# One-bank PSUM memories, ScalarE copies and an earlier search in a fused convolution and expert kernel

## The chip, the cores and the metric

The kernel runs as one launch on one core of a Trainium2 chip. The metric is the device time of an execution in microseconds (us). Five engines have an instruction queue of their own, each in order: TensorE (PE in the profile, its weight loads PEld), VectorE (DVE), ScalarE (ACT), GpSimd (POOL) and SyncE (SP), which issues nearly all transfers. Matrix products land in PSUM, which has eight banks of 512 fp32 numbers per partition; all other data lie in SBUF.

## The reference: a long convolution, then an expert for 128 rows

```python
Xf = np.fft.rfft(x, n=L, axis=1)            # x: 8 x 6336 x 128, L = 2 * 6336
y = np.fft.irfft(Xf * np.fft.rfft(h, n=L, axis=0)[None], n=L, axis=1)[:, :S, :]
...
scores = np.einsum('bsd,d->bs', y, w_gate)
top_idx = np.argpartition(-scores[b], 128)[:128]          # per batch b
ye = np.maximum(y[b, top_idx] @ w1, 0.0) @ w2             # 128 -> 1024 -> 128
out[b, top_idx] = y[b, top_idx] + sigmoid(scores)[:, None] * ye
```

Each of 128 channels is convolved with its own filter along 6336 positions. In each of the 8 batches the 128 positions of highest score then get a gated two-layer network added.

## The kernel before

6336 is 99 x 64, and the transforms are matrix products over the two factors. The work is cut into 8 **units** (`NU`): unit i holds two batches (pair i // 2) and half of the channels (i % 2). So an even unit and the odd one after it finish one pair. Each unit passes four stages, all in fp32:

- **A** (`stage_a`, L146): the n1 products, 8 groups, each two quarters q. A quarter is 16 matmuls into a PSUM tile `pb`, which two copies (L153 on ScalarE or L155 on VectorE, by a list of four flags) carry into the memory `ys`. Before it GpSimd folds the input (L133, L134, two operations a group).
- **B** (`stage_b`, L180, L189, L200): the n2 products, 13 chunks (12 of 8 columns, one of 3). A chunk is matmuls into `pb`, four VectorE multiplications with the filter's spectrum (L189) back into `ys` and a helper `tx`, and two GpSimd additions (L200). It needs a table chunk `wb` and a filter chunk `hd`, loaded three chunks ahead.
- **C** (`stage_c`, L262, L268): 66 steps s of up to four matmuls into `pa`, which ScalarE copies into `zs`. `zs` lies over the same memory as the unit's own `ys`.
- **D** (`stage_d`, L290, L295): 16 items of matmuls into `pa`, a ScalarE copy to `yt` and a store to the output.

Beside them runs the routing of each pair. `weigh` (L241) sums the 64 columns of a unit's `ys` with the gate's weights into `acc`, 64 VectorE operations. They are recorded inside stage C, up to five columns ahead of the step, and a copy into `zs` must wait for those whose columns it overwrites. When both units of a pair are summed, `scores` (L310) turns `acc` into scores; `pick` finds the 128th highest in 16 rounds, each a few VectorE operations (L356, L360, L363, L373) and one small matmul that sums counts over partitions (L368); then row numbers are made. When the pair's output is stored, `gather` (L458) fetches the rows by indirect transfers of GpSimd, and `feed` runs the network for the two batches (L469 to L497) and scatters the rows back.

**What sets the order.** The kernel is recorded under `manual_schedule`: each engine runs its instructions in the order in which the Python code makes them. The main loop over i takes 33 items: 17 from C (four steps each) and 16 from D. A table `plan` puts next unit's A ahead of items 1, 3, 5 and 7 (two groups each) and next unit's B ahead of items 10, 14, 18, 22, 26 and 30 (two chunks each, the last three). After each item `aside()` may advance the routing by one piece, if a modelled clock `t["pe"]` has passed the piece's due time (`after_dve`, `after_act`). The routing of a pair may start when the odd unit's C is over (`phase[1]`, item 17), and gather when the next unit begins. After unit 7 what is left of the routing runs alone.

PSUM is full: three one-bank `pa` buffers, two two-bank `pb` buffers and one bank `m` for the routing.

Of the kernel before, what the change touches and what calls it, by code (L numbers as in the profile page):

```python
# [32 lines left out]
def conv_moe(ctx, tc, x, h, wg_d, w1, w2, fa_d, wb_d, wc_d, at_d, wgl_d, tri_d, cst_d, tw_d, fb_d, out):  # L33
# [26 lines left out]
        return pa_.tile([128, 512], F32, tag="a", name="pa")  # L60

    def psb():
        return pb_.tile([128, 2, 512], F32, tag="b", name="pb")

    def psm():
        return pm_.tile([128, 512], F32, tag="m", name="m")
# [69 lines left out]
    def stage_a(g, r, engines):  # L136

        a, o = raw.pop(g), odd.pop(g)
        n = g % 8
        for q in range(2):  # L140
            pt = psb()
            for d in range(4):
                for b, c in ((0, 0), (1, 1), (0, 1), (1, 0)):
                    rows = slice(b * 64, b * 64 + NE)
                    src = (o if c else a[:, 0])[rows, q * 4 + d]
                    pe.matmul(pt[c * 64:c * 64 + 64, b, d * N1:(d + 1) * N1], src, fa[rows, c], start=True, stop=True)  # L146
            j = n * 4 + q * 2
            dst = ys[r].rearrange("p (b j) k t -> p b j t k", b=2)
            src = pt[:, :, 0:4 * N1].rearrange("p b (j t k) -> p b j t k", j=2, t=2)
            on_pe(0.7)  # L150
            for b in range(2):
                if engines[q * 2 + b]:
                    act.copy(out=dst[:, b, j:j + 2], in_=src[:, b])  # L153
                else:
                    v.tensor_copy(out=dst[:, b, j:j + 2], in_=src[:, b])  # L155
                    on_dve(0.5)

    kchunks = [(k, min(KC, N1 - k)) for k in range(0, N1, KC)]
# [44 lines left out]
    def stage_b(i, ci):  # L203
        r, u = i % 2, i % 2
        k0, kn = kchunks[ci]
        pt = psb()
        banks = [pt[:, 0], pt[:, 1]]
        over_k(r, wts.pop((r, ci)), ci, banks)
        ht = hts.pop((u, ci))
        times(r, ci, banks, [ht[:, 0, 0:kn], ht[:, 1, 0:kn]])  # L210
        load_w(r, ci + RW)
        load_h(u, ci + RH)

    def stage_b_first(ci):
# [7 lines left out]
        pt = psb()  # L222
        banks = [pt[:, 0], pt[:, 1]]
        over_k(0, wt, ci, banks)
        times(0, ci, banks, [hs[:, 0, 0, 0:kn], hs[:, 1, 0, 0:kn]])
        for u in range(2):
            sp.dma_start(out=hd[u, :, :, k0:k0 + kn], in_=hs[:, :, u, 0:kn])
        load_w(0, ci + RW)
# [11 lines left out]
        else:  # L240
            v.scalar_tensor_tensor(out=dst, in0=col, scalar=w, in1=dst, op0=ALU.mult, op1=ALU.add)  # L241

    def stage_c(i):
        r = i % 2
        y = ys[r].rearrange("p (j c) k t -> p j c k t", c=2)
        z = zs[r].rearrange("p (n g j) m t -> p n g j m t", g=2, j=2)
        banks = [None, None]
        weighed = 0
        for s in range(66):
            while weighed < min(64, s + 5):  # L250
                weigh(i, weighed)
                weighed += 1
            cols = [s, s - 2]
            for g in range(2):
                if 0 <= cols[g] < 64 and cols[g] % 4 == 0:
                    banks[g] = psa()
            for ri in range(2):
                for g in range(2):
                    c = cols[g]
                    if 0 <= c < 64:  # L260
                        rows = slice(g * 64, g * 64 + 64)
                        pe.matmul(banks[g][0:N1, c % 4 * 128:c % 4 * 128 + 128], y[rows, c // 2, ri, :, c % 2],  # L262
                                  wc[rows, ri], start=(ri == 0), stop=(ri == 1))
            on_pe(0.44)
            for g in range(2):
                c = cols[g]
                if 0 <= c < 64 and c % 4 == 3:
                    act.copy(out=z[:, c // 4, g].rearrange("p j m t -> p j t m"),  # L268
                             in_=banks[g][0:N1].rearrange("p (j t m) -> p j t m", j=2, t=2))
            if s % 4 == 3 or s == 65:  # L270
                yield

# [2 lines left out]
    def load_at(n):  # L275
        if n < 17:
            k = min(2, NT - 2 * n)
            ats[n] = tp.tile([N1, 2, 2, N1], F32, tag="at", name="at", bufs=RA)
            sp.dma_start(out=ats[n][:, 0:k], in_=at_d[:, 2 * n:2 * n + k])

    def stage_d(i):
        r, p, u = i % 2, i // 2, i % 2
        z = zs[r].rearrange("p j (c m) t -> p c m j t", c=2)
        for n in range(16):
            pt = psa()
            todo = [(0, 0, 1), (1, 1, 1), (2, 2, 2)] if n == 0 else [(2 * n + 1, 4 * n, 2), (2 * n + 2, 4 * n + 2, 2)]
            for tau, q, w in todo:
                o = q % 4 * 128
                for c in range(2):
                    pe.matmul(pt[0:N1, o:o + w * 128], ats[tau // 2][:, tau % 2, c], z[:, c, q:q + w],  # L290
                              start=(c == 0), stop=(c == 1))
                if tau % 2:
                    load_at(tau // 2 + RA)
            yt = tp.tile([N1, 2, 4, 64], F32, tag="y", name="yt", bufs=3)
            act.copy(out=yt.rearrange("p b q d -> p q b d"),  # L295
                     in_=pt[0:N1].rearrange("p (q b d) -> p q b d", q=4, b=2))
            on_pe(1.78)
            sp.dma_start(out=out[2 * p:2 * p + 2, u, :, 4 * n:4 * n + 4].rearrange("b a q d -> a b q d"), in_=yt)
            yield

# [163 lines left out]
    def feed(b0, got):  # L464
        ov = out[0:b0 + 2].rearrange("b u a q d -> (b u a q) d")
        for iu, xt in got:
# [11 lines left out]
            v.reciprocal(out=gg, in_=gg)  # L478
            hm = []
            for f0 in range(0, NF, 4):  # L480
                yield after_act(3.0)
                ph = psm().rearrange("p (f t) -> p f t", f=4)
                for f in range(4):
                    pe.matmul(ph[:, f], w1s[:, (f0 + f) * 128:(f0 + f + 1) * 128], xet, start=True, stop=True)  # L484
# [5 lines left out]
            yield after_act(3.0)  # L490
# [5 lines left out]
            for u in range(2):  # L496
                pool.indirect_dma_start(  # L497
                    out=ov, out_offset=bass.IndirectOffsetOnAxis(ap=iu[:, u:u + 1], axis=0),
                    in_=xt[:, u], in_offset=None)
            yield after_act(3.0)  # L500

    phase = [0, False]

    def route(p):
        b0 = 2 * p
        while phase[0] < 2 * p + 1 or not phase[1]:
            yield
        ss = yield from scores()
        picked = []
        yield from pick(b0, 2, ss, picked)  # L510
        while phase[0] < 2 * p + 2:
            yield
        got = gather(b0, picked)
        for n in range(4):
            yield
        yield from feed(b0, got)

    def all_routes():
# [10 lines left out]
    with tc.manual_schedule():  # L529
# [29 lines left out]
        fold(17, pool)  # L559

        for i in range(NU):
            phase[0], phase[1] = i, False
            if i < NU - 1:
                for ci in range(RW):
                    load_w((i + 1) % 2, ci)
            cs, ds = stage_c(i), stage_d(i)
            g0 = 16 + 8 * i
            plan = {}
            if i < NU - 1:
                for n in range(4):  # L570
                    plan.setdefault(1 + 2 * n, []).append(("a", 2 * n))
                for n in range(6):
                    plan.setdefault(10 + 4 * n, []).append(("b", 2 * n))
            for item in range(33):
                strand = cs if item < 17 else ds
                for kind, n in plan.get(item, []):
                    if kind == "a":
                        for g in (g0 + n, g0 + n + 1):
                            if g % 8 < 6:
                                fold(g + 2, pool)  # L580
                            elif g % 8 == 7:
                                fold(g + 1, pool)
                            stage_a(g, (i + 1) % 2, (1, 1, 0, 0))
                            load_x(g + RX)
                            if g % 8 == 7:
                                fold(g + 2, pool)
                    else:
                        for ci in (n, n + 1) if n < 10 else (10, 11, 12):
                            stage_b(i + 1, ci)
# [146 lines left out]
```

## Time and profile before

| what | value |
|---|---|
| three timed runs | 1099.97, 1106.51, 1111.1 us (median 1106.51) |
| the profiled execution | 1099.84 us; its span 1098.1 us, so 1.74 us lie around it |
| mean granted TensorE clock | 0.92 of full speed |
| start of unit 0's stage C | 116.3 us |
| end of unit 7's stage D | 1033.0 us |
| instructions | 39650 |
| moved by DMA | 170.81 MB, mean 156 GB/s |

The profile gives, for each engine, busy time and, for each idle stretch, the event that ended it. A group row reads: line, engine, operation, output<-inputs, shapes, count | busy us, mean ns of one | idle us before, and what ended it. A timeline row is start, duration, engine, line, operation, names, and in brackets the idle time just before. A fp32 matmul of the code is two MATMUL records in the profile (4096 of L262 for 2048 in the code); the instruction order counts it once.

### The profile page before, as it was taken

To read this page: it belongs to the slowest core of one execution; us is meant where nothing else is said; L and a number is where in the kernel's file an instruction comes from. 1 tells how busy PE (TensorE), PEld (TensorE's weight loads), DVE (VectorE), ACT (ScalarE), POOL (GpSimd) and SP (SyncE) were. 2 spreads that over 40 slices of the span, in tenths; PEclk is the share of its full clock that TensorE was granted. 3 is DMA by queue.
4 is the path that set the end of the run, shared out by engine and by line. 5 is a ranking of instruction groups with operands and counts; after the bars stand their busy time and mean duration, and the time that the engine had idled before them with its cause. 6 is when DMAs were issued, how large, how long until landed. Compare 5 with 4: busy or idle time off the path is not lost.

```text
span 1098.1 us, 39650 instructions
## 1 busy us (share of the span) xinstructions
PE 933.6 (85%) x17368; PEld 819.3 (75%) x17368; DVE 779.4 (71%) x1910; ACT 340.0 (31%) x619; POOL 481.6 (44%) x372
## 2 busy tenths in 40 slices
PE   5787799989998889988998789969998798999614
PEld 5687698879877787777877787769877697788514
DVE  5354777487778896787588796776768896791681
ACT  3522253235212431243223431234312441254101
POOL 7154754365335533654445443563436234420002
PEclk8899799999999999989999899989999898999856
DMA  6388545764466436563476346463465235513200
GB/s 254 118 269 281 190 136 159 250 221 136 132 210 196 135 117 221 153 206 100 125 229 200 114 124 202 149 207 109 134 196 166 93 89 183 173 51 98 87 0 10
DMA packets 102344, 170.81 MB, mean 156 GB/s; under 512 B 10814, under 2 KB 80028, under 8 KB 102172
## 3 DMA queue, kind: packets, MB, share of 16 engines
q1 hardware_dynamic: 101148, 167.24, 47.8%
q8 instruction: 136, 2.23, 0.8%
q0 software_dynamic: 1024, 1.05, 0.4%
q14 instruction: 36, 0.29, 0.1%
HBM read 135.29 MB, written 32.96 MB: 153 GB/s over the span
## 4 chain that ended last, share of the span: by engine, by line
PE 53%; DVE 36%; issue 5%; DMA 2%; ACT 2%; POOL 1%; POOLq 0%; ACTq 0%; SPq 0%; DVEq 0%
PE pa L290 14%; PE pa L262 13%; PE pb L180 12%; DVE acc L241 11%; PE pb L146 8%; DVE tx L189 6%; DVE slots L189 5%; DVE cmp L356 4%; DVE slots L155 2%; PE pa L180 2%; DVE num L360 2%; PE m L484 2%; PE m L493 2%; DVE r L363 1%; DMA out<-yt 1%
## 5 line engine op out<-in xcount | busy, mean ns | idle before, releaser
L200 POOL TENSOR_TENSOR slots<-slots,tx 128x512 f32<-128x512 f32 (+1 forms) x208 | 266.9, 1315 | 340.3 <-DVE tx L189 339.1
L262 PE MATMUL pa<-wc,slots 64*99 64x128 f32 x4096 | 276.5, 287 | 11.4 <-ACT slots L268 5.2
L262 PEld LDWEIGHTS pa<-wc,slots 64*99 64x99 f32 x4096 | 254.7, 177 | 24.8 <-issue 7.2
L290 PE MATMUL pa<-slots,at 99*99 99x256 f32 (+1 forms) x1056 | 244.3, 383 | 18.2 <-ACT slots L268 18.2
L241 DVE SCALAR_TENSOR_TENSOR acc<-slots,wgl,acc 128x198 f32<-128x198 f32 x496 | 241.4, 554 | 2.0 <-POOL slots L200 2.0
L268 ACT COPY slots<-pa 99x512 f32<-99x512 f32 x256 | 162.1, 634 | 244.9 <-PE pa L262 217.9
L180 PEld LDWEIGHTS pb<-slots 128*64 128x64 f32 x6336 | 198.7, 139 | 28.3 <-issue 18.4
L180 PE MATMUL pb<-slots 128*64 128x64 f32 x6336 | 207.4, 225 | 14.3 <-issue 9.0
L290 PEld LDWEIGHTS pa<-slots,at 99*99 99x99 f32 x1056 | 166.6, 167 | 68.8 <-ACT slots L268 19.9
L189 DVE TENSOR_TENSOR slots<-pb,ht 128x512 f32<-128x512 f32 (+1 forms) x182 | 119.4, 656 | 102.7 <-PE pb L180 95.7
L295 ACT COPY yt<-pa 99x512 f32<-99x512 f32 x128 | 75.0, 586 | 324.0 <-PE pa L290 191.3
L146 PE MATMUL pb<-fa,xr 50*64 50x99 f32 x2048 | 118.0, 263 | 55.1 <-DVE slots L155 43.5
L146 PEld LDWEIGHTS pb<-fa,xr 50*64 50x64 f32 x2048 | 100.9, 143 | 69.1 <-issue 46.7
L189 DVE TENSOR_TENSOR tx<-pb,ht 128x512 f32<-128x512 f32 (+1 forms) x182 | 118.8, 653 | 0.0
L155 DVE COPY slots<-pb 128x396 f32<-128x396 f32 x128 | 67.5, 564 | 66.7 <-PE pb L146 49.8
L153 ACT COPY slots<-pb 128x396 f32<-128x396 f32 x160 | 75.4, 524 | 68.3 <-PE pb L146 67.5
L133 POOL TENSOR_TENSOR two<-xr 128x512 f32<-128x512 f32 x42 | 55.4, 1319 | 62.8 <-PE pb L146 62.8
L134 POOL TENSOR_TENSOR xr<-xr 128x512 f32<-128x512 f32 x56 | 73.5, 1312 | 4.4
L146 PE MATMUL pb<-fa,two 50*64 50x99 f32 x1344 | 75.0, 258 | 0.0
L356 DVE SCALAR_TENSOR_TENSOR cmp<-r,q,quarters 99x192 bf16<-99x192 f32 x128 | 73.4, 614 | 0.3
L146 PE MATMUL pb<-fa,slots 50*64 50x99 f32 x1216 | 61.1, 293 | 11.9 <-DVE slots L134 8.3
L146 PEld LDWEIGHTS pb<-fa,slots 50*64 50x64 f32 x1216 | 53.1, 165 | 13.7 <-DVE slots L134 8.3
(100 smaller groups left out, 599.7 us busy)
## 6 DMA issues: line engine op xcount, KB each, us to landing
slots<-tab_wb SPq DMA_DIRECT2D x96, 512.0 KB
xr<-in_x SPq DMA_DIRECT2D x64, 512.0 KB
out<-yt SPq DMA_DIRECT2D x128, 198.0 KB
ht<-hd SPq DMA_DIRECT2D x84, 256.0 KB
at<-tab_at SPq DMA_DIRECT2D x128, 153.1 KB
hd<-slots SPq DMA_DIRECT2D x24, 256.0 KB
slots<-in_h SPq DMA_DIRECT2D x8, 512.0 KB
slots<-tab_wb SPq DMA_DIRECT2D x8, 192.0 KB
```

The source lines that it names most:

```text
L146: pe.matmul(pt[c * 64:c * 64 + 64, b, d * N1:(d + 1) * N1], src, fa[rows, c], start=True, stop=True)
L153: act.copy(out=dst[:, b, j:j + 2], in_=src[:, b])
L155: v.tensor_copy(out=dst[:, b, j:j + 2], in_=src[:, b])
L180: pe.matmul(banks[c][g * 64:g * 64 + 64, j * 64:j * 64 + 64], wt[:, j, c * 64:c * 64 + 64], y[:, :, g, :, k0 + j], start=True, stop=True)
L189: v.tensor_tensor(out=dst, in0=banks[c][:, 0:kn * 64].rearrange("p (k b j t) -> p k b j t", k=kn, b=2, t=2), in1=ht[t].rearrange("p k (j t ...
L200: pool.tensor_tensor(out=d3, in0=d3, in1=tx.rearrange("p k (j t) -> p k j t", t=2), op=ALU.add if c else ALU.subtract)
L241: v.scalar_tensor_tensor(out=dst, in0=col, scalar=w, in1=dst, op0=ALU.mult, op1=ALU.add)
L262: pe.matmul(banks[g][0:N1, c % 4 * 128:c % 4 * 128 + 128], y[rows, c // 2, ri, :, c % 2], wc[rows, ri], start=(ri == 0), stop=(ri == 1))
L268: act.copy(out=z[:, c // 4, g].rearrange("p j m t -> p j t m"), in_=banks[g][0:N1].rearrange("p (j t m) -> p j t m", j=2, t=2))
L290: pe.matmul(pt[0:N1, o:o + w * 128], ats[tau // 2][:, tau % 2, c], z[:, c, q:q + w], start=(c == 0), stop=(c == 1))
L295: act.copy(out=yt.rearrange("p b q d -> p q b d"), in_=pt[0:N1].rearrange("p (q b d) -> p q b d", q=4, b=2))
L356: v.scalar_tensor_tensor(out=cmp[:, j], in0=r[:, j].unsqueeze(1).broadcast_to([N1, 3, N2]), scalar=q[:, j:j + 1], in1=quarters[0:N1], op0= ...
```

## The change

1. `psb` gives two tiles of one bank each, with a name of its own per bank, in place of one tile of two banks. A, B and the prologue's B use them; the number of banks stays four.
2. In the main loop all four copies of an A group are on ScalarE (flags 1, 1, 1, 1); they were two on ScalarE and two on VectorE. The prologue's groups keep 1, 1, 1, 0.
3. The weighted sums of an odd unit leave its own stage C. They are recorded in the even unit before it, five after each item from 20 on, when that unit's items have already made all of the odd unit's B.
4. The routing of a pair may start at the beginning of the odd unit, no longer at its item 17.
5. B moves: in even units ahead of items 8, 10, 12, 14, 16, 17 (two chunks each) and 19 (one); in odd units ahead of 9, 13, 17, 20, 23, 26 (two each) and 29 (one).
6. `aside()` is called after every second step of C and inside every D item but the first, and no longer once per item. The due times of `feed` fall from 3.0 to 1.7 modelled us, a modelled 6.0 us stands between gather and feed in place of four items, and D's modelled cost is booked within the item.

```diff
     def psb():
-        return pb_.tile([128, 2, 512], F32, tag="b", name="pb")
+        return [pb_.tile([128, 512], F32, tag="b" + str(c), name="pb") for c in range(2)]
...
-                    pe.matmul(pt[c * 64:c * 64 + 64, b, d * N1:(d + 1) * N1], src, fa[rows, c], start=True, stop=True)
+                    pe.matmul(pt[b][c * 64:c * 64 + 64, d * N1:(d + 1) * N1], src, fa[rows, c], start=True, stop=True)
...
-        pt = psb()
-        banks = [pt[:, 0], pt[:, 1]]
+        banks = psb()
...
-    def stage_c(i):
+    def stage_c(i, weighing=True):
...
-            while weighed < min(64, s + 5):
+            while weighing and weighed < min(64, s + 5):
                 weigh(i, weighed)
...
+            if s % 2:
+                aside()
             if s % 4 == 3 or s == 65:
                 yield
...
+                on_pe(0.89)
+                if w == 2 and tau != 2:
+                    aside()
...
-            on_pe(1.78)
...
-                yield after_act(3.0)
+                yield after_act(1.7)
...
-        while phase[0] < 2 * p + 1 or not phase[1]:
+        while phase[0] < 2 * p + 1:
             yield
...
-        for n in range(4):
-            yield
+        yield after_act(6.0)
...
-            cs, ds = stage_c(i), stage_d(i)
+            cs, ds = stage_c(i, i % 2 == 0), stage_d(i)
...
-                for n in range(6):
-                    plan.setdefault(10 + 4 * n, []).append(("b", 2 * n))
+                for n, at_item in enumerate((8, 10, 12, 14, 16, 17, 19) if i % 2 == 0 else (9, 13, 17, 20, 23, 26, 29)):
+                    plan[at_item] = ("b", 2 * n, 2 if n < 6 else 1)
+            early = 0
...
-                            stage_a(g, (i + 1) % 2, (1, 1, 0, 0))
+                            stage_a(g, (i + 1) % 2, (1, 1, 1, 1))
...
-                if item == 17:
-                    phase[1] = True
+                if i % 2 == 0 and item > 19:
+                    for _ in range(5):
+                        if early < 64:
+                            weigh(i + 1, early)
+                            early += 1
                 next(strand, None)
-                aside()
```

Three places of the instruction order show it. Line numbers of the changed kernel are shifted a little: its L260, L239, L370, L397, L409, L417, L436 and L471 are L262, L241, L368, L395, L407, L415, L434 and L469 of the kernel before.

TensorE at the end of unit 7, before: the last D products (`pa<-slots,at`), then only the search's count sums.

```order
L368 LDWEIGHTS ones_87
L368 MATMUL m<-num,ones_87 99x6
L290 MATMUL pa<-slots,at 99x256 x4
L368 LDWEIGHTS ones_87
L368 MATMUL m<-num,ones_87 99x6
```

Fourteen further such pairs follow, and then the making of the row numbers. In the changed kernel the same place reads, with `cmp` and `lane` those of the row numbers and L471 the first instruction of `feed`:

```order
L290 MATMUL pa<-slots,at 99x256 x6
L436 LDWEIGHTS cmp
L436 MATMUL m<-lane_89,cmp 128x1
...
L290 MATMUL pa<-slots,at 99x256 x4
L436 LDWEIGHTS cmp
L436 MATMUL m<-lane_89,cmp 128x1
...
L438 MATMUL m<-hf,cmp 128x64
L471 MATMUL m<-tri,xe 128x128
L486 MATMUL m<-xet,w1s 128x128 x8
```

All 16 rounds of the last search now stand between earlier products of unit 7, and behind the last D product stand four small products for the second batch's row numbers.

VectorE in unit 0's stage C, where unit 1's A runs, before (`slots<-pb` are A's copies, `acc` the weighted sums):

```order
L239 TENSOR_SCALAR acc<-slots,wgl 128x198 x2
L241 SCALAR_TENSOR_TENSOR acc<-slots,wgl,acc 128x198 x6
L155 COPY slots<-pb 128x2x2x99 x4
L241 SCALAR_TENSOR_TENSOR acc<-slots,wgl,acc 128x198 x8
L155 COPY slots<-pb 128x2x2x99 x4
```

and now, through the first of five B pieces in the same stage:

```order
L237 TENSOR_SCALAR acc<-slots,wgl 128x198 x2
L239 SCALAR_TENSOR_TENSOR acc<-slots,wgl,acc 128x198 x30
L237 TENSOR_SCALAR acc<-slots,wgl 128x198 x2
L239 SCALAR_TENSOR_TENSOR acc<-slots,wgl,acc 128x198 x2
L189 TENSOR_TENSOR slots<-pb,ht 128x8x32x2
L189 TENSOR_TENSOR tx<-pb,ht 128x512
```

The copies are gone from this queue. Eight multiplications then alternate with eight sums three times, where before one such change was followed by sixteen sums.

VectorE at the end of unit 0, now: the last chunk's multiplications, the odd unit's sums, and the first operations behind `scores` of pair 0.

```order
L189 TENSOR_TENSOR slots<-pb,ht 128x3x32x2
L189 TENSOR_TENSOR tx<-pb,ht 128x192
L239 SCALAR_TENSOR_TENSOR acc<-slots,wgl,acc 128x198 x64
L318 TENSOR_TENSOR hf<-m,tw 99x128 x2
L318 TENSOR_TENSOR m<-m,tw 99x128 x2
L321 TENSOR_TENSOR half<-hf,m 99x128
```

On TensorE the same place holds the rest of unit 0's D, four products of unit 1's C, and then the eight of `scores` (L312), which read the result of all 64 sums:

```order
L180 MATMUL pb<-slots 64x64 x12
L290 MATMUL pa<-slots,at 99x256 x56
L260 MATMUL pa<-wc,slots 99x128 x4
L312 MATMUL m<-wc,acc 99x128 x8
L260 MATMUL pa<-wc,slots 99x128 x8
```

Before, the odd unit's sums stood in its own stage C and `scores` behind the first item of its D.

More of the change, by code (lines that the diff above doesn't have):

```diff
@@ L145, in stage_a @@
                     src = (o if c else a[:, 0])[rows, q * 4 + d]
-                    pe.matmul(pt[c * 64:c * 64 + 64, b, d * N1:(d + 1) * N1], src, fa[rows, c], start=True, stop=True)
+                    pe.matmul(pt[b][c * 64:c * 64 + 64, d * N1:(d + 1) * N1], src, fa[rows, c], start=True, stop=True)
             j = n * 4 + q * 2
             dst = ys[r].rearrange("p (b j) k t -> p b j t k", b=2)
-            src = pt[:, :, 0:4 * N1].rearrange("p b (j t k) -> p b j t k", j=2, t=2)
+            src = [w[:, 0:4 * N1].rearrange("p (j t k) -> p j t k", j=2, t=2) for w in pt]
             on_pe(0.7)
@@ L152, in stage_a @@
                 if engines[q * 2 + b]:
-                    act.copy(out=dst[:, b, j:j + 2], in_=src[:, b])
+                    act.copy(out=dst[:, b, j:j + 2], in_=src[b])
                 else:
-                    v.tensor_copy(out=dst[:, b, j:j + 2], in_=src[:, b])
+                    v.tensor_copy(out=dst[:, b, j:j + 2], in_=src[b])
                     on_dve(0.5)
@@ L221, in stage_b_first @@
             act.copy(out=hs[:, c, :, 0:kn], in_=banks[c][:, 0:kn * 64].rearrange("p (k u d) -> p u k d", u=2, d=32))
-        pt = psb()
-        banks = [pt[:, 0], pt[:, 1]]
+        banks = psb()
         over_k(0, wt, ci, banks)
@@ L489, in feed @@
                     hm += [r[:, 0], r[:, 1]]
-            yield after_act(3.0)
+            yield after_act(1.7)
             py = psm()
@@ L499, in feed @@
                     in_=xt[:, u], in_offset=None)
-            yield after_act(3.0)
-    phase = [0, False]
+            yield after_act(1.7)
+    phase = [0]
     def route(p):
         b0 = 2 * p
-        while phase[0] < 2 * p + 1 or not phase[1]:
+        while phase[0] < 2 * p + 1:
             yield
@@ L561, in conv_moe @@
         for i in range(NU):
-            phase[0], phase[1] = i, False
+            phase[0] = i
             if i < NU - 1:
@@ L570, in conv_moe @@
                 for n in range(4):
-                    plan.setdefault(1 + 2 * n, []).append(("a", 2 * n))
-                for n in range(6):
-                    plan.setdefault(10 + 4 * n, []).append(("b", 2 * n))
+                    plan[1 + 2 * n] = ("a", 2 * n, 2)
+                for n, at_item in enumerate((8, 10, 12, 14, 16, 17, 19) if i % 2 == 0 else (9, 13, 17, 20, 23, 26, 29)):
+                    plan[at_item] = ("b", 2 * n, 2 if n < 6 else 1)
+            early = 0
             for item in range(33):
                 strand = cs if item < 17 else ds
-                for kind, n in plan.get(item, []):
-                    if kind == "a":
-                        for g in (g0 + n, g0 + n + 1):
+                if item in plan:
+                    kind, n, w = plan[item]
+                    for k in range(n, n + w):
+                        if kind == "a":
+                            g = g0 + k
                             if g % 8 < 6:
@@ L586, in conv_moe @@
                                 fold(g + 2, pool)
-                    else:
-                        for ci in (n, n + 1) if n < 10 else (10, 11, 12):
-                            stage_b(i + 1, ci)
-                if item == 17:
-                    phase[1] = True
+                        else:
+                            stage_b(i + 1, k)
+                if i % 2 == 0 and item > 19:
[3 more added lines that the diff above has]
+                            early += 1
                 next(strand, None)
-                aside()
             for st in (cs, ds):
```

## The prediction

> **What bounds the kernel now.** The page first, for the load of each engine.
>
> ```profile
> span 1098.1 us, 39650 instructions
> PE 933.6 (85%) x17368; PEld 819.3 (75%) x17368; DVE 779.4 (71%) x1910; ACT 340.0 (31%) x619; POOL 481.6 (44%) x372
> ```
>
> TensorE (PE) leads, but is idle for 164 us. The view by windows, cut where unit 0's C begins and unit 7's D ends, says where (the third column is PE's busy time, the one behind POOL the granted clock):
>
> ```profile
> 0.00:116.30 116.30, 85.43 (x2609) 80.78 (x2609) 56.32 (x90) 38.06 (x75) 55.91 (x46) 0.90 0.66 226
> 116.30:1033.00 916.70, 828.89 (x14662) 723.42 (x14662) 685.12 (x1641) 297.99 (x531) 417.96 (x319) 0.95 0.50 157
> 1033.00:1098.10 65.10, 19.28 (x100) 15.07 (x98) 37.96 (x180) 3.95 (x13) 7.74 (x8) 0.60 0.03 9
> ```
>
> The units lose 88 us of PE, at a clock of 0.95; the last 65 us hold 19 us of PE work. The waits of PE within the units (us in total, times, longest):
>
> ```profile
> PE pb L146 <- DVE slots L155: 36.7, 14, 5.3
> PE pa L290 <- ACT slots L268: 18.2, 8, 3.9
> PE pb L146 <- issue: 8.5, 20, 0.8
> PE m L368 <- DVE num L360: 7.4, 11, 1.9
> PE pa L262 <- ACT slots L268: 5.2, 2, 3.9
> ```
>
> So stage A waits for VectorE's copies, and D's first product for C's last copy. The chain of waits names what is behind the latter, and what follows on PE:
>
> ```profile
> 619.23 3.67 PE pa L262 x32
> 623.07 1.95 PE pa L262 x32
> 626.95 1.85 PE pb L146 x64
> ...
> 655.26 2.84 DVE acc L241 x4
> 658.85 3.73 PE pa L290 x12
> ...
> 180.81 1.99 PE pa L290 x12
> 330.95 3.94 PE pb L180 x128
> 338.45 3.55 PE pa L290 x16
> 500.26 3.79 PE pa L262 x64
> ```
>
> The last four weighted sums hold up C's last copy, hence D. After a long wait PE runs at half rate: the same 32 products take 3.67 and then 1.95 us, D's first 12 take 3.73 or 1.99. The other rows are stage prices at full clock: a group of A 1.85, two chunks of B 3.94, an item of C 3.79 / 2 = 1.9, of D 3.55 / 2 = 1.8.
>
> **The end.** The timeline from D's last products:
>
> ```profile
> 1031.09 1.96 PE L290 MATMUL pa<-slots,at 99*99 99x256 f32 x8
> 1033.13 0.59 ACT L295 COPY yt<-pa 99x512 f32<-99x512 f32 x1 [1.57 <-PE m L368]
> 1036.56 0.24 PE L368 MATMUL m<-num,ones 99*99 99x6 bf16 x1 [1.64 <-DVE num L360]
> 1038.43 0.24 PE L368 MATMUL m<-num,ones 99*99 99x6 bf16 x1 [1.63 <-DVE num L360]
> 1069.31 0.98 POOL L458 DMA_INDIRECT xe<-out,iu  x1 [46.24 <-DVE col L447]
> 1073.15 0.44 PE L469 MATMUL m<-tri,xe 128*128 128x128 f32 x1 [2.06 <-DMA xe<-out,iu]
> 1073.95 2.08 PE L484 MATMUL m<-xet,w1s 128*128 128x128 f32 x8 [0.36 <-ACT xet L471]
> 1093.63 0.97 POOL L497 DMA_INDIRECT out<-xe,iu  x1 [1.44 <-DMA out<-xe,iu]
> ```
>
> A round alone takes 1.87 us (1036.56 to 1038.43). After the change the order leaves no round behind D. What remains: the last copy (to 1033.72), its store, a gather (1069.31 to 1073.15: 3.8), and from there to the end 25.0 unchanged. The store's landing is estimated by this row of the chain:
>
> ```profile
> 694.37 3.61 DMA out<-yt
> ```
>
> So the network would start at 1033.7 + 3.6 + 3.8 = 1041.1 in place of 1073.15: **-32**. The moved rounds cost PE about 0.2 us each in D (14 of them), **+3**. The first network of the end will run at half clock as now, since PE still pauses some 8 us.
>
> **A's copies.** The 36.7 us go: **-36.7**. In exchange ScalarE makes eight copies per piece of two groups, beside four of C:
>
> ```profile
> 610.41 0.93 ACT L153 COPY slots<-pb 128x396 f32<-128x396 f32 x2 [0.19 <-PE pb L146]
> L268 ACT COPY slots<-pa 99x512 f32<-99x512 f32 x256 | 162.1, 634 | 244.9 <-PE pa L262 217.9 <-DVE acc L241 23.6 <-DMA slots<-tab_wb 1.0
> ```
>
> That is 4 x 0.93 + 4 x 0.63 = 6.3 us, against 3.7 + 3.8 = 7.5 of PE. It fits, and C's copies, which stand behind A's on ScalarE, come 1 us late at most, with a third `pa` buffer as cover. But within a piece a quarter's two copies take as long (0.93) as its products (1.85 / 2), plus the 0.19 of hand-over. With two buffers, the third and fourth quarters wait some 0.3 us more than the "issue" waits already do; 28 pieces: **+8**. Bounds: 0 and 28 x 0.93 = 26; the low side, as the flags 1, 1 of the first quarter show waits of 0.4 only. Halving the PSUM tile alone is worth nothing: both banks of a quarter fill and empty together, and all four multiplications of B need both.
>
> **D's start.** In units 0 to 6 two chunks of B (3.94 us) now stand between C's last product and D's first, so the copy is hidden; unit 7 keeps 0.7: **-17.5** of 18.2. If VectorE were over 4 us late there, it would come back. The 3.9 in L262 was one copy into `zs` behind a step of the network on ScalarE; the new places make that rarer: **-3**.
>
> **Clock.** Half-rate pieces after these waits cost 1.7 us each (3.67 - 1.95, 3.73 - 1.99). Some 22 waits go, and the longest six to eight of them had paid it: **-11**, between 0 and -30.
>
> **B beside the sums, even units.** VectorE's rows, and GpSimd's beside one of them:
>
> ```profile
> 172.35 0.68 DVE L189 TENSOR_TENSOR slots<-pb,ht 128x512 f32<-128x512 f32 x1
> 177.14 2.92 DVE L241 SCALAR_TENSOR_TENSOR acc<-slots,wgl,acc 128x198 f32<-128x198 f32 x4
> 165.44 6.99 DVE L241 SCALAR_TENSOR_TENSOR acc<-slots,wgl,acc 128x198 f32<-128x198 f32 x16
> 512.97 3.69 DVE L241 SCALAR_TENSOR_TENSOR acc<-slots,wgl,acc 128x198 f32<-128x198 f32 x4
> 510.16 5.26 POOL L200 TENSOR_TENSOR slots<-slots,tx 128x512 f32<-128x512 f32 x4
> ```
>
> Eight multiplications take 177.14 - 172.35 = 4.8 us, a sum 6.99 / 16 = 0.44 alone and up to 3.69 / 4 = 0.92 beside GpSimd. Two items with B now ask 4.8 + 8 x 0.44 = 8.3 of VectorE (with four slow sums 10.2) and 3.94 + 3.8 = 7.7 of PE. So VectorE falls behind by 0.6 to 2.5 us a round, three rounds and a half; two chunks of buffer swallow about 3 us: a stall of 0 to 7 an even unit. I take 3.5: **+14** for four.
>
> The Trainium skill (SBUF — State Buffer, section "Who interferes with whom") says that a VectorE instruction with two SBUF inputs and a GpSimd instruction that reads SBUF exclude one another for a whole instruction. The trace agrees: 3.69 us beside L200 against 0.44 each without. By that rule alone all eight sums of a round would run at 0.92, 12.2 us a round, and this term would be some 60 us; but GpSimd's four additions end in 5.3, and only the first few sums meet them.
>
> **The odd unit's sums.** 64 x 0.44 = 28 us must fit into 13 items of D, 13 x 1.8 = 23.4, and 0.5 of C; GpSimd has nothing there. They begin with the last chunk's additions, about as item 20 starts. `scores` then stops PE for 28 - 24 = 4 us; at 0.42, as the fastest rows, for 3. Four units at 3.5: **+14**. Behind `scores` on PE wait all of C and A.
>
> **Gather and folds.** Gather now stands on GpSimd's queue at the head of units 2, 4 and 6, waiting for the store (3.6), then four gathers and the folds that A needs:
>
> ```profile
> L458 POOL DMA_INDIRECT xe<-out,iu x16 | 21.9, 1370 | 70.4 <-DVE col L447 67.6 <-DVE acc L241 0.9 <-DVE cmp L427 0.6
> L134 POOL TENSOR_TENSOR xr<-xr 128x512 f32<-128x512 f32 x56 | 73.5, 1312 | 4.4
> ```
>
> 3.6 + 4 x 1.37 + 2 x 1.31 = 11.7 us until the third group is folded; PE asks for it after three items of C and a piece of A, 9.4. **+7** for three units.
>
> **Search in C.** A round finds 24 products (48 records, 3.79 x 48 / 64 = 2.8 us) between its PE steps, against 1.87 alone; beside the folds it is slower. Of 64 waits, bounded by 0 and the longest row (1.9), I take 14 us in all in place of 7.4: **+7**.
>
> **Sum** against the profiled 1099.84: gains 32 + 36.7 + 17.5 + 3 + 11 = 100; costs 3 + 8 + 14 + 14 + 7 + 7 = 53. That gives 1053. I forecast **1052** for the timed runs: the profiled execution is the lowest of those shown (median 1106.51, 0.6% higher), but two of my costs, the C stall and the copies, are set on the careful side.
>
> **The rivals.**
>
> *Everything new is hidden* (0.17). With half the costs, and 11 to 20 of clock: 1099.84 - 100 + 26 = 1026 down to 1017. For it: VectorE loses 112 of the copies below (7 units x 16), 63 us of its queue. Against: the sums in D exceed its length by any row.
>
> ```profile
> L155 DVE COPY slots<-pb 128x396 f32<-128x396 f32 x128 | 67.5, 564 | 66.7 <-PE pb L146 49.8 <-ACT slots L153 16.8
> ```
>
>
> *VectorE binds the second half of C* (0.2). At 10.2 us a round the lag is 2.5 x 3.5 = 9 an even unit: +22 over my 14, 1074. For it: 512.97. Against: units 2, 4 and 6 also hold the network's 9 us of PE there.
>
> *Slower* (0.03): the 64 sums in D run at 0.92 all through. That is 59 us against 24, a stall of 35 in each of four units, +126 over my 14: 1178. It decides from 0.61 us a sum: 64 x 0.61 - 24 = 15, 12 over my 3.5, and four times that is the whole gain of 47. Against it: the order has no GpSimd work between the last addition and the next unit's first fold or gather.
>
> *The search does not finish in unit 7* (0.04): if its rounds stall, the end shrinks by half only, 1068. *B's loads bind* (0.05):
>
> ```profile
> slots<-tab_wb SPq DMA_DIRECT2D x96, 512.0 KB
> ht<-hd SPq DMA_DIRECT2D x84, 256.0 KB
> ```
>
> In even units' C ten chunks of these two in 39 us are 200 GB/s, where the units' mean was 157; at that mean 11 us more an even unit, 1096. SP issues them in order, each when the chunk three before it is used up, so a late one holds up the next. Against it: the first window moved 226 GB/s.
>
> **Chances.** My forecast 0.51. Faster by over 1% (about what a measurement of this kernel can tell from none): the forecast, the hidden case, VectorE bound and the unfinished search, 0.92; the loads' case is the rest within 1%, 0.05; slower 0.03. The range 1020 to 1084 reaches into the hidden case and takes in the VectorE one.
>
> **What would show it.** Right: L155 has no wait left in the units; the last 65 us become about 33; PE's waits on L268 before L290 nearly vanish; a wait of 3 to 4 us ahead of L312 in units 1, 3, 5 and 7. Wrong: PE waiting on L189 for over 30 us in all, an L312 wait of 10 us or more, A pieces over 4.5 us, or count rounds of the last search behind D.

## The result and the profile after

| kernel | timed runs | median |
|---|---|---|
| before | 4, 1099.97 to 1111.1 us | 1106.07 us |
| changed | 4, 1011.68 to 1017.91 us | 1015.98 us |

The ratio is 0.918, 95% interval 0.913 to 0.924: 90 us faster. The forecast of 1052 was 36 us too high, and the time lies 4 us below the range. The direction was right; the sizes of several terms were not. 1016 is just under the times of the rival "everything new is hidden" (1017 to 1026, given 0.17).

The page of the changed kernel first. TensorE (PE) does the same work in a span 82 us shorter, and VectorE has lost the 112 copies:

```profile
span 1015.8 us, 39643 instructions
PE 932.7 (92%) x17368; PEld 815.6 (80%) x17368; DVE 715.7 (70%) x1798; ACT 387.4 (38%) x731; POOL 466.4 (46%) x372
```

The view by windows, cut at the same two events as before (start of unit 0's C, end of unit 7's D; columns as in the prediction):

```profile
0.00:118.40 118.40, 87.68 (x2609) 82.12 (x2609) 57.48 (x90) 36.79 (x75) 56.37 (x46) 0.94 0.64 222
118.40:979.50 861.10, 827.76 (x14690) 718.74 (x14690) 653.42 (x1688) 346.64 (x643) 402.25 (x319) 0.98 0.54 167
979.50:1015.80 36.30, 17.24 (x70) 14.71 (x70) 4.80 (x21) 3.95 (x13) 7.74 (x8) 0.58 0.06 16
```

The units took 916.7 us and now 861.1: 55.6 less, where the terms of the prediction add up to 15.2 less. The end took 65.1 and now 36.3: 28.8 less, with 32 predicted. The first stretch is 2.1 longer. PE's busy time within the units has hardly moved (828.9, now 827.8), so by the profile's account nearly all of their gain is idle time: 87.8 us before, 33.3 now.

PE's waits from 113 to 1000 us in the changed kernel, that is the units and the first 20 us of the end:

```profile
PE m L471 <- DMA xe<-out,iu: 15.9, 4, 6.3
PE m L370 <- DVE num L362: 11.9, 13, 1.8
PE pb L180 <- DVE slots L189: 3.7, 4, 1.7
PE pa L260 <- POOL slots L200: 3.4, 1, 3.4
PE pb L180 <- issue: 3.3, 2, 1.7
PE pb L180 <- DVE tx L189: 2.4, 9, 0.3
...
PE pa L290 <- ACT slots L266: 0.7, 1, 0.7
```

Compare this list with the one in the prediction. The first three entries of before (36.7 for VectorE's copies, 18.2 ahead of D, 8.5 of "issue" in stage A) are gone or down to 0.7. What leads now is new: the network's wait for its rows (15.9, of which 6.3 is the end and 9.6 lies in units 2, 4 and 6) and the search's count sums. B's waits together are 9.4, against 5.3 in the same view of before.

The end, in the timeline of the changed kernel:

```profile
979.53 0.58 ACT L298 COPY yt<-pa 99x512 f32<-99x512 f32 x1 [1.31 <-PE pa L290]
983.28 0.98 POOL L460 DMA_INDIRECT xe<-out,iu  x1 [93.21 <-DVE iu L451]
987.16 0.45 PE L471 MATMUL m<-tri,xe 128*128 128x128 f32 x1 [6.34 <-DMA xe<-out,iu]
```

No round of the search stands between D and the gather any more. From the last copy to the network's first product it takes 7.0 us (the prediction's 3.6 + 3.8 = 7.4).

### The profile page after: what moved, and what is told of

The parts are those of the page before. It is cut to its first block, busy times and chain, and to the rows that moved or that the text cites. A ratio compares the mean times of both kernels' runs of the same rounds, so it can differ in the third digit from the quotient of the medians.

```text
span 1015.8 us, 39643 instructions
## 1 busy us (share of the span) xinstructions
PE 932.7 (92%) x17368; PEld 815.6 (80%) x17368; DVE 715.7 (70%) x1798; ACT 387.4 (38%) x731; POOL 466.4 (46%) x372
## 4 chain that ended last, share of the span: by engine, by line
PE 66%; DVE 23%; DMA 5%; issue 4%; POOL 1%; ACT 0%; POOLq 0%; SPq 0%; ACTq 0%; DVEq 0%
PE pa L290 17%; PE pa L260 16%; PE pb L146 12%; PE pb L180 11%; DVE tx L189 7%; DVE slots L189 5%; DVE acc L239 5%; PE pa L180 2%; PE m L486 2%; DMA xe<-out,iu 2%; PE m L495 2%; DVE cmp L358 2%; DMA xr<-in_x 1%; PE m L312 1%; DVE num L362 1%
## 5 line engine op out<-in xcount | busy, mean ns | idle before, releaser
L260 PE MATMUL pa<-wc,slots 64*99 64x128 f32 x4096 | 270.8, 278 | 3.4 <-POOL slots L200 3.4
L260 PEld LDWEIGHTS pa<-wc,slots 64*99 64x99 f32 x4096 | 242.6, 168 | 22.4 <-ACT slots L266 3.9
L239 DVE SCALAR_TENSOR_TENSOR acc<-slots,wgl,acc 128x198 f32<-128x198 f32 x496 | 231.7, 541 | 3.4 <-POOL slots L200 3.4
L290 PE MATMUL pa<-slots,at 99*99 99x256 f32 (+1 forms) x1056 | 232.4, 374 | 0.7 <-ACT slots L266 0.7
L180 PE MATMUL pb<-slots 128*64 128x64 f32 x6336 | 211.9, 226 | 19.9 <-issue 13.6
L153 ACT COPY slots<-pb 128x396 f32<-128x396 f32 x272 | 122.0, 533 | 53.4 <-PE pb L146 53.3
L146 PE MATMUL pb<-fa,xr 50*64 50x99 f32 x2048 | 127.0, 266 | 0.7 <-issue 0.5
L146 PEld LDWEIGHTS pb<-fa,xr 50*64 50x64 f32 x2048 | 106.4, 145 | 14.7 <-issue 10.2
L133 POOL TENSOR_TENSOR slots<-xr 128x512 f32<-128x512 f32 x22 | 29.4, 1344 | 103.4 <-PE pa L290 67.6
L460 POOL DMA_INDIRECT xe<-out,iu x16 | 15.4, 963 | 124.4 <-DVE iu L451 93.2
```

Of the source, the lines that this page charges most:

```text
L133: pool.tensor_tensor(out=odd[g], in0=a[:, 1], in1=a[:, 0], op=ALU.subtract)
L146: pe.matmul(pt[b][c * 64:c * 64 + 64, d * N1:(d + 1) * N1], src, fa[rows, c], start=True, stop=True)
L153: act.copy(out=dst[:, b, j:j + 2], in_=src[b])
L180: pe.matmul(banks[c][g * 64:g * 64 + 64, j * 64:j * 64 + 64], wt[:, j, c * 64:c * 64 + 64], y[:, :, g, :, k0 + j], start=True, stop=True)
```

## The experiments

Two questions were open. Where do the 40 us come from by which the units beat the forecast: from ScalarE's copies alone, or from costs that did not come? And was the price of a weighted sum, on which three terms and the one slower rival rest, read rightly? The expectations name their own theories. All times are medians of four timed runs (five for the changed kernel with one two-bank tile, six for the last two kernels); each ratio is to the kernel before, run on the same chip at the same time (1103.27, 1100.14 and 1104.06 us in the three groups).

### The copies alone, put into the kernel before

```diff
-                            stage_a(g, (i + 1) % 2, (1, 1, 0, 0))
+                            stage_a(g, (i + 1) % 2, (1, 1, 1, 1))
```

> The kernel before with all four copies on ScalarE in the main loop, nothing else. Theory 1: the 36.7 us of waits on VectorE's copies go, and some 10 us of half clock: 1106 - 45 = 1060 us. Rival (ScalarE's copies into a joint tile bind A): A blocks over 4.2 us, 1075 us or more.

Measured: 1059.4 us, ratio 0.960 [0.953, 0.968]: 44 us from four flags, as theory 1 had it. PE's waits in this kernel:

```profile
PE pa L290 <- ACT slots L268: 21.4, 8, 4.2
...
PE pb L146 <- POOL xr L134: 9.2, 8, 3.6
PE pb L146 <- issue: 6.0, 15, 0.4
```

The wait on L155 is gone. That on C's last copy ahead of D stays (18.2, now 21.4), as it should: its cause is another.

### The copies and the split, in the kernel before

The previous edit, and `psb` with two one-bank tiles as in the change.

> The kernel before with ScalarE copies and one-bank tiles, nothing else. Theory 1: the same as ScalarE copies alone, within 4 us. Theory 2: at least 10 us below ScalarE copies alone, the A blocks 0.4 us shorter.

Measured: 1054.91 us, 0.957 [0.951, 0.962]. The 4.5 us below the previous kernel are less than the two intervals tell apart, though the "issue" waits of stage A fell from 6.0 to 0.9. Those waits did not turn into time: A's products within the units keep PE busy for 105.5 us here and for 96.1 in the previous kernel, and from one item of C to the next, with a piece of A between them, it takes 7.40 us here and 7.43 there. The A pieces are not 0.4 us shorter, as theory 2 would have them.

### The change without ScalarE's copies

```diff
-                            stage_a(g, (i + 1) % 2, (1, 1, 1, 1))
+                            stage_a(g, (i + 1) % 2, (1, 1, 0, 0))
```

> The changed kernel with two of a group's four copies on VectorE again. Theory 1 (VectorE's queue, with sums and search ahead of the copies, made A wait): 1016 + about 35 = 1050 us, with over 20 us of TensorE waits on these copies. Rival (with the odd unit's sums gone from C and the search spread, the copies would do no harm on VectorE): 1020 us, waits on these copies under 6 us.

Measured: 1026.36 us, 0.931 [0.926, 0.936]; only 10 us more than the changed kernel. That is nearer to the rival (1020, waits under 6 us) than to theory 1 (1050), and neither hit it. The row that differs most:

```profile
PE pb L146 <- DVE slots L155: 8.0, 7, 3.8
```

So the copies are worth 44 us in the kernel before and 10 in the changed one. The rest of the change, the one-bank tiles among it, takes away 28.7 of the 36.7 us by itself. Two parts of it remove the same wait, and their worths do not add. Which part of the rest does it was not run alone; the instruction order before showed A's copies among eight weighted sums a step, and the odd unit's sums no longer stand there, which fits.

### The change with one two-bank tile

```diff
-        return [pb_.tile([128, 512], F32, tag="b" + str(c), name="pb") for c in range(2)]
+        t2 = pb_.tile([128, 2, 512], F32, tag="b", name="pb")
+        return [t2[:, 0], t2[:, 1]]
```

> The changed kernel with one PSUM tile of two banks again, all else kept. Theory 1 (the ScalarE copies alone end stage A's waits, the split is worth nothing): 1016 us within 4, A blocks of two groups at 3.7 us. Theory 2 (the split lets TensorE refill a bank while the other is copied, which keeps ScalarE in pace): the 0.4 us wait of the kernel before returns in each of 28 blocks and grows, 1028 us or more.

Measured: 1016.19 us, 0.922 [0.917, 0.926]: the time of the changed kernel, as theory 1 had it. Yet the waits are there again:

```profile
PE pb L147 <- issue: 7.0, 17, 0.4
PE pb L147 <- ACT slots L154: 2.2, 6, 0.4
```

What such a wait costs is read from the time between two items of C with a piece of A (two groups) between them, first in the changed kernel, then with the two-bank tile (L260 and L261 are C's products):

```profile
134.30 3.86 PE L260 MATMUL pa<-wc,slots 64*99 64x128 f32 x64
141.70 3.86 PE L260 MATMUL pa<-wc,slots 64*99 64x128 f32 x64
```

```profile
132.17 3.85 PE L261 MATMUL pa<-wc,slots 64*99 64x128 f32 x64
139.61 3.86 PE L261 MATMUL pa<-wc,slots 64*99 64x128 f32 x64
```

It is 7.40 us without a listed wait and 7.44 with one of 0.4, so 28 pieces cost about 1 us. With one-bank tiles the same time stands in the products instead: A's products within the units keep PE busy for 110.4 us in the changed kernel and for 103.0 here. The wait has left the list, but hardly shortened the stage.

The changed kernel was run again, unaltered, in the second group:

> The changed kernel itself, unaltered, as the yardstick of this call: 1012 to 1018 us by both theories.

Measured: 1016.38 us, 0.922 [0.917, 0.927]. Its profile warns against reading single waits too finely. L471 waits only at the end here, and 7.4 us of "issue" stand in its place at stage A, all of them in pieces at the start of units 2, 4 and 6, where the first profile has the network's waits:

```profile
PE pb L146 <- issue: 7.4, 14, 1.1
PE m L471 <- DMA xe<-out,iu: 6.3, 1, 6.3
```

Its end took 32.6 us where that of the first profile took 36.3. Between executions of one program, terms of a few us change place.

### The odd unit's sums back in their own stage

The scores then cannot come before item 17 of the odd unit, so the search starts late again as well.

```diff
-            cs, ds = stage_c(i, i % 2 == 0), stage_d(i)
+            cs, ds = stage_c(i), stage_d(i)
...
-                if i % 2 == 0 and item > 19:
-                    for _ in range(5):
-                        if early < 64:
-                            weigh(i + 1, early)
-                            early += 1
+                if item == 17:
+                    phase[1] = True
...
-        while phase[0] < 2 * p + 1:
+        while phase[0] < 2 * p + 1 or not phase[1]:
```

> The changed kernel with the odd unit's sums in its own stage C again and the routing from item 17 of the odd unit; all else kept, B's places too. Eight rounds and the row numbers then stand behind the last D product: 8 x 1.87 + 6.5 = 21 us. Theory 1 (moving the sums also takes them away from the folds): the units lose another 10 us or more, with waits on C's copies in odd units, 1048 us. Rival (the move is worth the end alone): 1038 us.

Measured: 1041.76 us, 0.946 [0.942, 0.951], 25 us more than the changed kernel and nearer to the rival's 1038 than to theory 1's 1048. The windows show the end:

```profile
984.40:1038.70 54.30, 20.11 (x92) 16.38 (x92) 25.32 (x116) 3.95 (x13) 7.75 (x8) 0.59 0.04 11
```

54.3 us against 32.6 to 36.3: eight rounds of the search are behind D again. That is 18 to 22 of the 25 us. From the start of unit 0's C, at 115.0 us, the units take 869.4 us, 3 to 8 more than in the two profiles of the change (866.0 and 861.1). PE waits there 15.7 us for folded input, which those two do not show, and 9.5 for B's multiplications (3.7 in the first):

```profile
PE pb L146 <- POOL xr L134: 15.7, 7, 6.1
...
PE pb L180 <- DVE slots L189: 9.5, 12, 2.1
```

PE's idle time in the units is 55 us against 32 and 33, but its busy time is lower too (814.5 us; 833.7 and 827.8), so that little of the difference is left in the time. Why the products took less is open. C's last copies, of which theory 1 spoke, hold PE for 3.8 us only.

### GpSimd work beside the odd unit's sums

The changed kernel, with 17 additions on GpSimd per even unit beside the 64 sums. They add a memory of zeros to itself, and nothing reads the result; nothing waits for them by program.

```diff
                 if i % 2 == 0 and item > 19:
+                    for _ in range(1 + (item % 3 == 0)):
+                        pool.tensor_tensor(out=spare, in0=spare, in1=spare, op=ALU.add)
```

> The changed kernel with 17 additions on GpSimd (128 x 512, on a spare tile whose result nothing reads) recorded beside the 64 sums in the D stage of each even unit. Theory 1 (a sum takes 0.34 us alone and about 0.8 beside a GpSimd operation, and D hid the sums only because GpSimd is idle there): the sums take some 45 us in place of 21.6, scores holds TensorE for 15 to 20 us in units 1, 3, 5 and 7, 1016 + 70 = 1085 us. Rival (a sum's price is set by its own work and by VectorE's queue, as the prediction's 0.44 had it): under 1022 us.

Measured: 1067.2 us, 0.969 [0.965, 0.974]: 51 us more, from 68 additions that depend on nothing. The timeline at unit 0's D, first of the changed kernel and then of this one (L241, L597 and L314 are here the sums, the additions and `scores`):

```profile
202.08 21.57 DVE L239 SCALAR_TENSOR_TENSOR acc<-slots,wgl,acc 128x198 f32<-128x198 f32 x64 [0.85 <-POOL slots L200]
225.46 1.99 PE L312 MATMUL m<-wc,acc 128*99 128x128 f32 x16
227.48 0.49 DVE L318 TENSOR_TENSOR hf<-m,tw 99x128 f32<-99x128 f32 x2 [3.84 <-PE m L312]
```

```profile
197.49 18.96 POOL L597 TENSOR_TENSOR spare<-spare 128x512 f32<-128x512 f32 x17
197.57 34.87 DVE L241 SCALAR_TENSOR_TENSOR acc<-slots,wgl,acc 128x198 f32<-128x198 f32 x64 [0.85 <-POOL slots L202]
220.04 13.52 POOL L135 TENSOR_TENSOR slots<-xr 128x512 f32<-128x512 f32 x1 [3.59 <-PE pa L292]
232.16 2.03 PE L314 MATMUL m<-wc,acc 128*99 128x128 f32 x8 [9.50 <-DVE acc L241]
```

Alone, 64 sums take 21.57 us, 0.337 each. They end at 223.65, and `scores` begins 1.8 us later without a wait, in all four odd units: the stall that the prediction placed here does not exist. (VectorE's 3.84 us of idle time are these 1.8 and the 2.0 of L312.) With the additions they take 34.87 us, and `scores` waits 9.5 us; in the four odd units that makes 39.6 of the 51 us. Another 8 us are in PE's busy time within the units (841.5 us, 833.7 in the second profile of the change), at a clock of 0.96 in place of 0.98. Theory 1 had the mechanism and was too high in size: 45 us for the sums and 1085 us in all. The same group of sums, split at the end of the additions:

```profile
L241 DVE SCALAR_TENSOR_TENSOR acc<-slots,wgl,acc 128x198 f32<-128x198 f32 x17 | 19.1, 1197 | 0.9 <-POOL slots L202 0.9
```

17 sums during 17 additions, one for one, 18.96 / 17 = 1.12 us a pair; the other 47 follow at (34.87 - 19.1) / 47 = 0.336. A sum alone is 0.337, so beside GpSimd's additions it costs the whole length of one. This is the exclusion that the Trainium skill states (SBUF — State Buffer, "Who interferes with whom"): a VectorE instruction with two SBUF inputs and a GpSimd instruction that reads SBUF contend through the shared read port. The rows agree. The prediction's rival "slower", in which the 64 sums run beside GpSimd, had its mechanism right: it decides from 0.61 us a sum, and a sum can cost 1.12. GpSimd has no work there in the changed kernel, as the prediction had read from the order.

### The two waits that the change leaves

In units 2, 4 and 6 the network waits for its rows, and in the odd units the search's sums come late. This kernel gives the network a later due time, and books 2 us more for VectorE ahead of the first round:

```diff
+        on_dve(2.0)
         bits = ss.bitcast(I32)
...
-        yield after_act(6.0)
+        yield after_act(10.0)
```

> The changed kernel with feed due 10.0 modelled us after gather in place of 6.0, and 2.0 us more booked for VectorE before the search's first round. Theory 1 (TensorE is the bound, so each wait taken off it is time won): the waits of L471 on the gathered rows (9.6 us in units 2, 4, 6) and of the first count sums (some 5 us) go and the time falls by 10 us, to 1006. Rival (these waits are made up elsewhere, by the loads or by VectorE): 1014 to 1018 us.

Measured: 1005.02 us, 0.912 [0.908, 0.916], 11 us less than the unaltered change beside it, as theory 1 had it. L471's wait in the units is gone, the count sums' fell from 11.9 to 4.3, and a new one has come that theory 1 did not foresee:

```profile
PE pb L146 <- POOL xr L134: 13.9, 3, 4.7
PE m L472 <- DMA xe<-out,iu: 6.3, 1, 6.3
PE m L371 <- DVE num L363: 4.3, 10, 0.7
```

GpSimd's timeline at the start of unit 2 says why:

```profile
332.26 3.46 POOL L461 DMA_INDIRECT xe<-out,iu  x1 [10.42 <-DMA ht<-hd]
...
338.53 0.94 POOL L461 DMA_INDIRECT xe<-out,iu  x1 [0.30 <-issue]
339.49 1.28 POOL L133 TENSOR_TENSOR slots<-xr 128x512 f32<-128x512 f32 x1
340.85 1.26 POOL L134 TENSOR_TENSOR xr<-xr 128x512 f32<-128x512 f32 x1
```

The four gathers hold up the first folds, and A waits 4.7 us for them (4.6 in units 4 and 6). That is the step that the prediction had named for its term of the folds. In the changed kernel it cannot be seen, because the network stands ahead of that A piece on PE and waits longer.

### The gathers behind the first folds

```diff
         while phase[0] < 2 * p + 2:
             yield
+        yield after_act(3.0)
         got = gather(b0, picked)
         yield after_act(10.0)
```

> The change with the network's due time at 10 and the search booked for 2 us more, as in the run before, and with the gathers recorded behind the first two folds of the next groups (due 3 us after the unit's start) instead of ahead of all folds on GpSimd. Theory (the three waits of 4.6 us for folded input in units 2, 4 and 6 are the folds standing behind four gathers that wait for the store): those waits go, L471 has none either since the network is due 13 us after the unit's start, and the time is 1005 minus 10 to 14, so 990 to 997. Rival (the loss only moves again, to the third piece of stage A or to the network): the fold wait comes back at the next piece or L471 waits again, and the time is 1002 to 1008.

The edit is to the kernel just before. Measured: 990.18 us, 0.897 [0.893, 0.900], 15 us less again and within the theory's range. In GpSimd's timeline folds now stand first, and the fold wait fell from 13.9 to 6.2 us:

```profile
328.92 1.27 POOL L133 TENSOR_TENSOR slots<-xr 128x512 f32<-128x512 f32 x1 [6.38 <-PE pa L290]
...
335.36 1.11 POOL L461 DMA_INDIRECT xe<-out,iu  x1 [0.16 <-DMA ht<-hd]
```

```profile
PE m L472 <- DMA xe<-out,iu: 6.3, 1, 6.3
PE pb L146 <- POOL xr L134: 6.2, 5, 1.9
PE m L371 <- DVE num L363: 4.7, 11, 0.6
```

The units take 839.1 us of the span of 986.5, at a clock of 0.99; in the kernel just before they took 856.7 at 0.98. Of these 17.6 us, 11.4 are PE's busy time (826.9, now 815.5): a long wait costs more than its length. The A piece behind the wait of 4.7 us took 5.5 us, one without a wait takes 3.6. What is left in this list is the wait at the end, the folds', now five short ones, and the count sums'.

### The same with one two-bank tile

> The kernel of the previous run with the two PSUM tiles of one bank joined again into one tile of two banks, all copies on ScalarE. If separate banks are worth something once the other waits are gone: the products of stage A wait about 0.4 us at two refills a piece, 28 pieces, so some 10 us of waits more and a time 5 to 10 us above the run with separate banks. If the halves fill and empty together and nothing on the path depends on it, as the prediction said: within 3 us of it.

Measured: 998.26 us, 0.903 [0.899, 0.907]: 8 us more, six runs from 992.5 to 1003.4 against 988.5 to 993.0. The intervals of the ratios still overlap a little. The waits of stage A's refills are back:

```profile
PE pb L147 <- issue: 12.7, 22, 2.0
```

The size is what the first expectation said, but its reason does not hold. Of the 22 waits 18 are of 0.4 us, with six more on ScalarE's copies, and a piece with such a wait is no longer than before: 7.44 us from one item of C to the next, 7.41 with one-bank tiles. A's products are shorter in return, 96.1 us against 103.5. The other four waits, of 0.9 to 2.0 us, make 5 us; whether they come with the two-bank tile or differ between executions, these runs do not show. What costs the 8 us stays open.

## Why the prediction was right in sign and wrong in size

Its terms, beside what the profile after gives. The measured column is the difference of PE's waits between the two profiles; for the end and the start it is that of the window, and for A and the clock PE's busy time is added (A's products 101.6 us before and 110.4 after, all of PE's in the units 828.9 and 827.8).

| term | predicted | measured |
|---|---|---|
| the end | -32 | -28.8 (-32.5 in the second execution) |
| A's copies and ScalarE's pace | -36.7 + 8 | -38.1 (-46.9 in waits, +8.8 in the products' own time) |
| D's start | -17.5 | -17.5 |
| L262's waits | -3 | -7.8 |
| B beside the sums | +14 | +4.1 |
| the odd unit's sums | +14 | 0 |
| gather and folds | +7 | +9.6 |
| search in C | +7 | +4.5 |
| clock and moved rounds | -11 + 3 | -9.9 (the rest of PE's busy time in the units) |
| start of the units | 0 | +2.1 |

Summed: -81.8, and the span fell by 82.3. The terms of the prediction add up to -47. The largest misses are the odd unit's sums (14), B (9.9) and A's copies (9.4). Not everything new was hidden, as that rival would have it: B's waits, the network's and the search's came, in part.

**What held.** The two waits named as removable went, that ahead of D by 17.5 us as predicted. The end came out as worked, 7.0 us from the last copy to the network. The mechanism of contention held too.

**The step that failed: the price of a sum alone.** The prediction took 6.99 / 16 = 0.44 us from the row at 165.44 and called it "alone". GpSimd's timeline of the kernel before, at that place, shows that it was not:

```profile
162.10 5.40 POOL L200 TENSOR_TENSOR slots<-slots,tx 128x512 f32<-128x512 f32 x4 [5.99 <-DVE tx L189]
```

GpSimd works until 167.5, the first 2 of the 7 us. Taken apart in the trace, the row holds two sums that take 2.2 us together and fourteen that follow at 0.335 each: the row is explained, and a sum alone is 0.337. The 0.42 of the "fastest rows" does not hold either: a single sum's record lasts 0.41 to 0.43 us, but the next one starts after 0.335. 64 of them are 21.6 us, not 28, and fit into D with 1.8 us to spare. So the term of 14 is zero, and the wait of 3 to 4 us announced ahead of L312 is not there. With it falls the argument that kept the hidden case at 0.17, that the sums in D exceed its length by any row.

**B beside the sums: right in mechanism, high in size.** Here the price of 0.44 was not too high but a little low, as GpSimd works beside the sums. VectorE in unit 0's C of the changed kernel, at the first multiplication of a round, its sums and the first of the next round:

```profile
153.24 0.69 DVE L189 TENSOR_TENSOR slots<-pb,ht 128x512 f32<-128x512 f32 x1 [6.24 <-issue]
...
158.03 4.32 DVE L239 SCALAR_TENSOR_TENSOR acc<-slots,wgl,acc 128x198 f32<-128x198 f32 x8
162.28 0.68 DVE L189 TENSOR_TENSOR slots<-pb,ht 128x512 f32<-128x512 f32 x1
```

Eight sums take 4.25 us, 0.53 each, and a round 9.04, where PE's round takes 7.72 (its B pieces begin at 151.04 and 158.76). VectorE falls behind by 1.3 us a round, inside the 0.6 to 2.5 worked out. PE's waits in B come in the even units alone, 2.1 to 2.7 us in each, 9.4 in all, where 3.5 each and 14 were taken. The 4.1 of the table are what is left when the 5.3 us of waits in B before, which the prediction did not list, are taken off.

**The second one: ScalarE's pace.** The prediction set two copies at 0.93, the length of a row, plus 0.19 of hand-over, hence 8 us of waits in A. ScalarE's timeline of the changed kernel:

```profile
131.64 1.77 ACT L153 COPY slots<-pb 128x396 f32<-128x396 f32 x4 [0.21 <-PE pb L146]
```

A row of four takes 1.77 us, so two further copies add 0.84, not 0.93: a row's length includes the whole last copy (0.53 on average), while a copy starts about 0.41 after the one before it. A quarter's two copies need 0.84 and its products 0.92, so ScalarE keeps up: a piece of A takes 3.6 us (7.40 less the 3.79 of an item of C), and the 8 us did not come. The "issue" waits of before (8.5) are at 0.5 in this profile, but 8.8 us more in A's products stand against that. "Halving the PSUM tile alone is worth nothing" held in the changed kernel (1016.19 against 1016.38 us) and, within the noise, in the kernel before (4.5 us). Only the fastest kernel shows 8 us, and the 0.4 us waits do not account for them.

**The clock.** C's and D's products were faster, 17.6 us in all, where 11 had been predicted for the units. The groups of D show its part, before and after:

```profile
L290 PE MATMUL pa<-slots,at 99*99 99x256 f32 (+1 forms) x1056 | 244.3, 383 | 18.2 <-ACT slots L268 18.2
```

```profile
L290 PE MATMUL pa<-slots,at 99*99 99x256 f32 (+1 forms) x1056 | 232.4, 374 | 0.7 <-ACT slots L266 0.7
```

A's and B's records grew by 13 us in the same execution, so PE's busy time is nearly as it was. Within the units 8.8 of the 13 are A's. That comes with the one-bank tiles: in all three pairs of kernels that differ in the tile alone, A's products take 7.4 to 9.4 us more with them, and the listed waits at its refills all but vanish. What lengthened B's is open.

**Right by its sum, not by its place: gather and folds.** The stall came, 9.6 us for the 7 predicted, but as the network's wait. In the second execution the network does not wait there, and A has its 7.4 us of "issue" instead. The wait of the folds, which the prediction worked out, lay behind it and came to light when the network was moved. Search in C (+7, measured 4.5) was sized well.

**The terms did not add.** The prediction booked the 36.7 us to the copies alone. In the kernel before they are theirs (44 us by four flags). In the changed order the other parts alone remove most of them.

## What to carry to other kernels

Before a duration from a profile is called "alone", look at what the other engine of a contending pair does in that same stretch; one row of 16 instructions can hold two prices. A wait that leaves the list is a gain only if the stage gets shorter: measure from the start of one stage to the start of the next, since the wait may have gone into the instructions' own time. When two edits remove the same wait, measure one of them in both kernels, since its worth in one says little about the other. And after a change that removes waits, read the list again: 26 us more came here from three lines that set the order, part of them from a wait that stood hidden behind another, and part from products that no longer run slowly behind long waits.

## What the runs showed of the hardware

- VectorE's two-input sums and GpSimd's additions, both queued without a break, alternate one for one (1.12 us a pair). But a single fold that arrived in a running row of sums took 13.52 us where it takes 1.27 otherwise: it ended 1.1 us after the sums did. What decides between the two patterns these runs do not show; that the fold came alone, while the additions stood ready from before the first sum, is the visible difference.
- Work that nothing waits for is not free: 68 additions of 1.1 us made the kernel 51 us slower.
- A row's duration is not the pace of a queue: ScalarE's copy of 128x396 reads 0.53 us on average in its group and follows its predecessor after 0.41 ((1.77 - 0.53) / 3); a VectorE sum reads 0.41 to 0.43 us and follows after 0.335.
- With one two-bank PSUM tile stage A shows waits of 0.4 us at its refills, with two one-bank tiles hardly any, but a piece takes the same time within 0.04 us (7.44 against 7.40 from one item of C to the next): the time of the waits stands in its products' records instead.
